# A decode block of attention and gated layer on one core: short on-chip loops on every engine, and the model dimension in four chunks of 112

## The chip, the cores and the metric

One core of a Trainium2 chip runs the whole program. The metric is the device time of one execution in microseconds, the median over several runs; a profiled execution gives the trace. Engines are named as the profile names them: PE (matmuls), DVE (vector), ACT (activations), POOL, and SP, which here only issues loads.

## What is computed

A pre-norm decode step for B = 2 rows with one new token each: attention over a cache of 8192 keys and values for 16 heads of 256, then a gated layer without a nonlinearity. Model dimension D = 448, inner dimension F = 1792, everything in float32.

```python
def _A_ref(x, k_cache, v_cache, wq, wo):
    q = (x @ wq).reshape(B, Sq, H, Dh).transpose(0, 2, 1, 3)
    scores = jnp.einsum("bhqd,bhkd->bhqk", q, k_cache) * (Dh ** -0.5)
    p = _softmax(scores, axis=-1)
    o = jnp.einsum("bhqk,bhkd->bhqd", p, v_cache)
    return o.transpose(0, 2, 1, 3).reshape(B, Sq, H * Dh) @ wo

def _B_ref(x, w_gate, w_up, w_down):
    h = jnp.einsum("bsd,df->bsf", x, w_gate) * jnp.einsum("bsd,df->bsf", x, w_up)
    return jnp.einsum("bsf,fd->bsd", h, w_down)

h = x + _A_ref(_layernorm(x), A_k_cache, A_v_cache, A_wq, A_wo)
h2 = h + _B_ref(_layernorm(h), B_w_gate, B_w_up, B_w_down)
```

Keys and values are 2 x 16 x 8192 x 256 numbers each, 537 MB of 4-byte numbers in sum; all weights together are much less. Every one of them is read once.

## The kernel before, in words

**A turn.** There are NQ = 32 pairs of head and row, called i in the code. For each, 8192 keys lie on 128 partitions, 64 a partition. DVE multiplies the keys with the query, which is spread to all partitions, in place (L334) and adds up along the 256 (L337), both in two pieces of HC = 16 and 48 keys a partition; then it takes the maximum per partition (L381). PE turns that column (L422), DVE takes the maximum of it (L343), PE spreads it (L426), ACT makes the exponentials p and their sums (L355), PE adds those up (L431), DVE takes the reciprocal (L348). The mix (L413) is 32 matmuls of two columns of p with 512 numbers of v, into four column groups of PE; ACT copies the result (L363), PE folds it (L438), and ACT scales it into oT (L365).

**Buffers and order.** Keys have two buffers, values have one (`v_sb`). SP issues all large loads in the order of the program (L383 to L393): keys i+1 once DVE has the maxima of i-1, then values i once PE has ended the mix of i-1. They are carried out one after the other. wq lies in the buffer of the values at first, so the first values wait for the last matmul of the query projection (L282).

**Programs.** `Line` gives an engine its instructions one by one, so DVE, ACT and SP have the 32 turns written out. `Tensor` records PE's instructions and emits 31 turns as one loop on the chip (L446 to L453), with waits on `turn * by + n`. Turn 31 stands behind the loop.

**The last turn and the rest.** wo is loaded into the buffer of the keys once the maxima of turn 30 are there, and PE adds heads 0 to 14 times wo onto x in a bank of PSUM (`acc_ps`, L493). DVE copies the sums (L513), and PE puts them into two other banks (L523): `h_ps`, from which the second norm is made, and `y_ps`, the output. The last values come in two loads of LASTV = 48 and 16 keys a partition. The last head's product with wo is then added to `h_ps` (L589) and, later, to `y_ps` (L697). The norm's mean and its subtraction go through DVE, ACT and PE (L597 to L620), and DVE spreads the result to `xr` (L630). Gate (L668) and up (L668, in two halves) follow, their product (L717), its turn (L720, L727), and the product with wd into `y_ps` (L738), which DVE copies (L747) and SP stores. The loads of gate, up and wd stand last on SP's queue: gate and up wait for the maxima of turn 31 (L469), wd for the first 48 of the last mix (L547).

**Chunks.** D = 448 is three chunks of 128 and one of 64. So that loads have 128 partitions, the host puts the 64-row chunk of one half of the columns on partitions 0 to 63 and that of the other half on 64 to 127; `LAYOUT` and a fifth column of `xr` and `xz` with zeros serve this.

Of the kernel before, what the change touches and what calls it, by code (L numbers as in the profile page):

```python
# [9 lines left out]
EPS = 1e-5  # L10
P = 128
HALF = 64
DC = 4
YN, YW = 4, D // 4
# [7 lines left out]
LASTV = 48  # L22

FG = (512, 512, 384, 384)
FO = (0, 512, 1024, 1408)
NF = F // P
FH = FG[0] // 2
WIDE = [[min(n, (k + 1) * FH) - k * FH for n in FG] for k in range(2)]
PACKED = [3 * sum(n) + n[0] + n[2] for n in WIDE]
# [3 lines left out]
LAYOUT = (  # L33
    (slice(0, P), slice(0, DC - 1), slice(0, DC - 1)),
    (slice(0, HALF), slice(DC - 1, DC), slice(DC - 1, DC)),
    (slice(HALF, P), slice(DC - 1, DC), slice(DC, DC + 1)),
)


class Line:  # L40


    def __init__(self, nc, engine, name):
        self.e = engine
        self.sem = nc.alloc_semaphore(name=name)
        self.n = 0
        self.seen = {}

    def wait(self, *tokens):
        for sem, n in tokens:  # L50
            if self.seen.get(sem.num, 0) < n:
                self.e.wait_ge(sem, n)
                self.seen[sem.num] = n

    def did(self, ins):
        ins.then_inc(self.sem, 1)
        self.n += 1
        return self.sem, self.n


class Tensor:


    def __init__(self, nc):
        self.e = nc.tensor
        self.sem = nc.alloc_semaphore(name="pe")
        self.n = 0
        self.parts = [(None, [])]

    def loop(self, *turns):  # L70

        self.parts.append((turns or None, []))

    def do(self, make, *waits, inc=False):
        self.parts[-1][1].append((make, waits, inc))
        if inc:
            self.n += 1
            return self.sem, self.n

    def emit(self):  # L80
        for turns, ops in self.parts:
            if turns:
                with self.e.Fori(*turns) as turn:
                    self.emit_part(ops, turn)
            else:
                self.emit_part(ops, None)

    def emit_part(self, ops, turn):
        seen = {}
        for make, waits, inc in ops:  # L90
            for w in waits:
                sem, n = w[:2]
                if len(w) == 3:
                    self.e.wait_ge(sem, turn * w[2] + n)
                elif seen.get(sem.num, 0) < n:
                    self.e.wait_ge(sem, n)
                    seen[sem.num] = n
            ins = make() if turn is None else make(turn)
            if inc:
                ins.then_inc(self.sem, 1)  # L100


def decode_block(nc, x, k_cache, v_cache, wq, wo, wg, wu, wd, out):
# [6 lines left out]
    bank = [nc.alloc_psum_tensor(f"bank{i}", [P, 512], F32)[:] for i in range(8)]  # L110
    first_sem = nc.alloc_semaphore(name="dve_first")
    V = Line(nc, nc.vector, "dve")
    A = Line(nc, nc.scalar, "act")
    A_q = Line(nc, nc.scalar, "act_q")
    G = Line(nc, nc.gpsimd, "pool")
    S = Line(nc, nc.sync, "sp")
    T = Tensor(nc)

# [3 lines left out]
    def load(line, dst, src, sem, n=16):  # L122
        line.e.dma_start(dst, src).then_inc(sem, 16)  # L123
        return sem, n
# [5 lines left out]

    room = {"at": 2 * NF * D}

    def late(*shape):

        n = 1
        for k in shape[1:]:
            n *= k
        at = room["at"]
        room["at"] += -(-n // 8) * 8
        assert room["at"] <= NJ * DH  # L140
        got = k_flat[1][: shape[0], at : at + n]
# [15 lines left out]
    xr = sb("xr", P, DC + 1, B, 16)  # L157
    xz = sb("xz", P, DC + 1, B)
    sel = sb("sel", P, 2)
    rep = sb("rep", P, 2, B, REP)  # L160
    q_sb = sb("q_all", B, H * DH)

    s_x, s_wq, s_k0 = landing("x"), landing("wq"), landing("k0")
    s_k = [landing("k_even"), landing("k_odd")]
    s_v, s_v2 = landing("v"), landing("v_last")
    s_wo = [landing("wo_a"), landing("wo_b")]
    s_wg, s_wu = landing("wg"), [landing("wu_a"), landing("wu_b")]
    s_wd = [landing(f"wd{i}") for i in range(len(DOWN))]
    s_out = landing("out")
# [7 lines left out]
    x_in = load(A, x_sb, x.rearrange("b s d -> (b s) d"), s_x)  # L177
    wq_t = v_flat[:, : 3 * H * DH + H * DH // 2]
    wq_in = load(S, wq_t, wq, s_wq)
    k0_in = load(S, k_sb[0][:, :HC], keys_of(k_cache, 0, 0, HC), s_k0)  # L180
    k_in = {0: load(S, k_sb[0][:, HC:], keys_of(k_cache, 0, HC, NJ), s_k[0])}
    k_in[1] = load(S, k_sb[1], keys_of(k_cache, 1, 0, NJ), s_k[1])

    zero = G.did(nc.gpsimd.memset(ident, 0.0))
    G.wait(zero)
    ident_in = G.did(
        nc.gpsimd.affine_select(
            out=ident, in_=ident, compare_op=ALU.not_equal, fill=1.0, base=0,
            pattern=[[-1, P]], channel_multiplier=1,
        )  # L190
    )
    G.did(nc.gpsimd.memset(xz, 0.0))
    zeros_in = G.did(nc.gpsimd.memset(xr[:, DC - 1 :], 0.0))

    V.did(nc.vector.memset(eps_t, EPS))
    V.did(nc.vector.memset(ones, 1.0))
    V.did(nc.vector.memset(avg, 1.0 / D))
    V.did(nc.vector.memset(row, DH**-0.5))
    o_ps, h_ps, y_ps = bank[0], bank[5][:, :P], bank[6][:, :YW]
    V.wait(x_in)  # L200
    xsum = sb("xsum", B, 1)
    t = V.did(nc.vector.tensor_reduce(xsum, x_sb, axis=AX.X, op=ALU.add))
    V.wait(t)
    xmean = sb("xmean", B, 1)
    t = V.did(nc.vector.tensor_scalar(xmean, xsum, -1.0 / D, None, op0=ALU.mult))
    V.wait(t)
    xc_sb = sb("xc", B, DC * P)
    t = V.did(nc.vector.tensor_scalar(xc_sb[:, :D], x_sb, xmean, None, op0=ALU.add))
    V.wait(t)
    xc_in = V.did(nc.vector.tensor_copy(xc_sb[:, D:], xc_sb[:, D - HALF : D]))  # L210
    xq = o_sb[:B, :D]
    t = V.did(nc.vector.tensor_mul(xq, xc_sb[:, :D], xc_sb[:, :D]))
    V.wait(t)
    xvar = sb("xvar", B, 1)
    var_in = V.did(nc.vector.tensor_reduce(xvar, xq, axis=AX.X, op=ALU.add))

    std = sb("std", B, 1)
    A.wait(var_in)
    std_in = A.did(nc.scalar.activation(std, xvar, AF.Sqrt, bias=eps_t, scale=1.0 / D))
    rstd = sb("rstd", B, 1)  # L220
    V.wait(std_in)
    rstd_in = V.did(nc.vector.reciprocal(rstd, std))
    A.wait(rstd_in)
    A.did(nc.scalar.activation(std, std, AF.Exp, scale=0.0))

    xT_ps = bank[3][:, : DC * B].rearrange("p (c b) -> p c b", b=B)
    for c in range(DC):
        xT_in = T.do(
            lambda c=c: nc.tensor.transpose(
                xT_ps[:, c, :], xc_sb[:, c * P : (c + 1) * P], ident[:B, :B]  # L230
            ),
            ident_in, xc_in, inc=c == DC - 1,
        )
    V.wait(xT_in, zeros_in)
    for rows, c, to in LAYOUT:
        xz_in = V.did(nc.vector.tensor_copy(xz[rows, to], xT_ps[rows, c]))

    V.wait(ident_in)
    V.did(
        nc.vector.tensor_reduce(  # L240
            sel, ident.rearrange("p (g r) -> p r g", r=32)[:, :2, :], axis=AX.X, op=ALU.add
        )
    )
    V.did(
        nc.vector.tensor_copy(
# [4 lines left out]
    for ps in (o_ps, h_ps, bank[4][:, :HW]):  # L250
        set_in = V.did(nc.vector.memset(ps, 0.0))

    q_sel = sb("q_sel", B, DH)
    qb = [sb(f"qb{i}", P, DH) for i in range(2)]
    qb_ps = bank[1][:, :DH]
    q_ps = [bank[7][:B, :], bank[4][:B, :]]
    qsel_in, qb_in, Q_in = {}, {}, {}

    def select(i):
        h, b = divmod(i % NQ, B)  # L260
        if i > 0:
            A.wait(Q_in[i - 1])
        qsel_in[i] = A_q.did(
            nc.scalar.activation(  # L264
                q_sel, q_sb[:, h * DH : (h + 1) * DH], AF.Copy, scale=ident[:B, b : b + 1]
            )
        )

    def spread_query(*_):
        return nc.tensor.matmul(qb_ps, ones[:B, :], q_sel, start=True, stop=True)  # L270

    def take_query(i):
        A.wait(Q_in[i])
        qb_in[i] = A_q.did(nc.scalar.activation(qb[i % 2], qb_ps, AF.Copy))  # L274

    q_in = {}
    for g in range(NG):
        for c in range(DC):
            xs = c if c < DC - 1 else c + g // (NG // 2)
            at = c * H * DH + (g * QG if c < DC - 1 else g % (NG // 2) * QG)  # L280
            done = T.do(
# [536 lines left out]
```

## Time and profile before

| what | value |
|---|---|
| runs, median of 3 | 1302.09 us (1301.49 to 1303.19) |
| profiled execution, its own time | 1301.42 us |
| its span, first to last instruction | 1300.1 us |
| busy: DVE, PE, ACT | 1131.2 us (87%), 470.6 us (36%), 81.5 us (6%) |
| HBM read | 561.19 MB |

In a row of groups stand: line, engine, operation, output and inputs by tile, shapes, how many; behind the first bar the busy time in us and the mean of one in ns; behind the second the idle time of the engine just before them in us and what ended most of it. PEld is PE's loading of weights, SPq the issuing of a load. One float32 matmul of the program shows as two MATMULs and two weight loads. In the timeline the idle time ahead stands in brackets.

### The profile page before, as it was taken

Reading aid. Unit: us, or ns where it says so; the run is one execution under the profiler, and the core shown is the slowest. Engines: PE = TensorE matmul, PEld = TensorE weight load, DVE = VectorE, ACT = ScalarE, POOL = GpSimd, SP = SyncE. Lnnn points to the kernel's source line nnn. Section 1 sums busy time; section 2 is a strip of 40 time slices with the busy share of each in tenths; the row PEclk is TensorE's granted clock in tenths of the full one; section 3 lists DMA queues with packets and bytes.
Section 4 is the critical chain, followed back from the end, with each engine's and each line's share of the span. In section 5 each row is a group of like instructions: output and inputs, shape, how many; then the busy total and the mean of one; then the engine's idle time right before and its main releaser. Section 6 shows DMA issues by size and latency. Waiting matters only on the chain.

```text
span 1300.1 us, 6914 instructions
## 1 busy us (share of the span) xinstructions
PE 470.6 (36%) x2992; PEld 155.1 (12%) x2992; DVE 1131.2 (87%) x266; ACT 81.5 (6%) x239; POOL 0.8 (0%) x8
## 2 busy tenths in 40 slices
PE   3643224333323433322333322333321333432387
PEld 0111011101001101101101101101100110110123
DVE  1999998889888889888889988888988888988861
ACT  1100000000000000000000000000000000000000
POOL 0000000000000000000000000000000000000000
PEclk9866566666556666556666656666656666655689
DMA  9999999999999999999999999999999999999998
GB/s 411 427 450 421 450 421 444 426 436 436 421 450 421 448 423 448 423 446 425 442 427 427 444 421 450 422 446 425 446 423 446 425 440 429 427 444 423 446 421 367
DMA packets 10973, 561.31 MB, mean 432 GB/s; under 512 B 1234, under 2 KB 1364, under 8 KB 1492
## 3 DMA queue, kind: packets, MB, share of 16 engines
q1 hardware_dynamic: 10960, 561.19, 99.7%
q8 instruction: 5, 0.08, 0.0%
q14 instruction: 4, 0.03, 0.0%
q10 hardware_dynamic: 4, 0.00, 0.0%
HBM read 561.19 MB, written 0.00 MB: 432 GB/s over the span
## 4 chain that ended last, share of the span: by engine, by line
DMA 74%; PE 25%; issue 0%; ACT 0%; SPq 0%; DVE 0%
DMA v<-in_A_v_cache_dram 71%; PE bank L413 22%; PE bank L282 2%; DMA v<-in_wd_dram 2%; DMA v<-in_wq_dram 1%; PE bank L270 0%; SPq L123 0%; PE bank L738 0%; ACT q_all L290 0%; ACT q_sel L264 0%; DVE k L747 0%; ACT qb L274 0%
## 5 line engine op out<-in xcount | busy, mean ns | idle before, releaser
L334 DVE TENSOR_TENSOR k<-k,qb 128x4096 f32<-128x4096 f32 x64 | 555.3, 8676 | 124.2 <-DMA k<-in_A_k_cache_dram 95.9
L337 DVE TENSOR_REDUCE s<-k 128x16 f32<-128x4096 f32 x64 | 555.2, 8675 | 1.1
L413 PE MATMUL bank<-v,p 128*2 128x512 f32 x2048 | 291.4, 733 | 342.9 <-DMA v<-in_A_v_cache_dram 342.9
L413 PEld LDWEIGHTS bank<-v,p 128*2 128x2 f32 x2048 | 53.6, 96 | 573.4 <-DMA v<-in_A_v_cache_dram 365.9
L426 PE MATMUL bank<-nm,row 1*128 1x1 f32 x64 | 18.4, 354 | 227.6 <-DVE nm L343 227.6
L422 PE MATMUL bank<-ident,m 128*1 128x128 f32 x32 | 11.8, 368 | 184.4 <-DVE m L381 184.4
L363 ACT ACTIVATE o_sb<-bank 128x512 f32<-128x512 f32 x31 | 18.5, 597 | 604.0 <-PE bank L413 604.0
L426 PEld LDWEIGHTS bank<-nm,row 1*128 1x128 f32 x64 | 15.6, 302 | 236.9 <-DVE nm L343 236.9
L438 PE MATMUL bank<-sel,o_sb 128*128 128x1 f32 x256 | 33.7, 253 | 23.3 <-ACT o_sb L363 22.5
L270 PE MATMUL bank<-q_sel,ones 2*128 2x256 f32 x66 | 39.0, 691 | 1.4 <-ACT q_sel L264 1.4
L438 PEld LDWEIGHTS bank<-sel,o_sb 128*128 128x128 f32 x256 | 31.0, 191 | 53.1 <-ACT o_sb L363 51.5
L282 PE MATMUL bank<-v,xz 128*2 128x512 f32 x64 | 30.7, 639 | 16.0 <-DMA v<-in_wq_dram 16.0
L352 ACT ACTIVATE nb<-bank 128x1 f32<-128x1 f32 x32 | 5.5, 171 | 441.5 <-PE bank L426 441.5
L431 PE MATMUL bank<-lsum,ones 128*128 128x1 f32 x64 | 18.5, 359 | 23.5 <-ACT p L355 23.5
L422 PEld LDWEIGHTS bank<-ident,m 128*1 128x1 f32 x32 | 2.5, 79 | 188.2 <-DVE m L381 187.8
L431 PEld LDWEIGHTS bank<-lsum,ones 128*128 128x128 f32 x64 | 15.8, 306 | 26.2 <-ACT p L355 26.2
L270 PEld LDWEIGHTS bank<-q_sel,ones 2*128 2x128 f32 x66 | 15.9, 297 | 3.7 <-ACT q_sel L264 2.4
L264 ACT ACTIVATE q_sel<-q_all,ident 2x256 f32<-2x256 f32 x33 | 16.2, 492 | 0.0
L274 ACT ACTIVATE qb<-bank 128x256 f32<-128x256 f32 x32 | 12.2, 382 | 54.5 <-PE bank L270 54.5
L493 PE MATMUL bank<-k,oT 128*2 128x224 f32 x120 | 13.4, 387 | 0.0
L343 DVE TENSOR_REDUCE nm<-bank 1x1 f32<-1x128 f32 x32 | 8.7, 272 | 4.4 <-PE bank L422 4.4
L597 DVE TENSOR_REDUCE k<-bank 128x1 f32<-128x128 f32 x1 | 0.3, 292 | 13.1 <-PE bank L589 13.1
(81 smaller groups left out, 97.3 us busy)
## 6 DMA issues: line engine op xcount, KB each, us to landing
v<-in_wq_dram SPq DMA_DIRECT2D x1, 7168.0 KB, 19.5
k<-in_wo_dram SPq DMA_DIRECT2D x2, 3584.0 KB, 35.3
k<-in_A_k_cache_dram SPq DMA_DIRECT2D x1, 6144.0 KB, 38.0
v<-in_A_v_cache_dram SPq DMA_DIRECT2D x1, 6144.0 KB, 21.6
k<-in_wg_dram SPq DMA_DIRECT2D x1, 3136.0 KB, 28.0
v<-in_wd_dram SPq DMA_DIRECT2D x2, 1120.0 KB, 18.0
k<-in_A_k_cache_dram SPq DMA_DIRECT2D x1, 2048.0 KB, 23.9
v<-in_A_v_cache_dram SPq DMA_DIRECT2D x1, 2048.0 KB, 26.1
```

What stands on the lines that cost most here:

```text
L264: nc.scalar.activation(q_sel, q_sb[:, h * DH : (h + 1) * DH], AF.Copy, scale=ident[:B, b : b + 1])
L270: return nc.tensor.matmul(qb_ps, ones[:B, :], q_sel, start=True, stop=True)
L282: lambda g=g, c=c, xs=xs, at=at: nc.tensor.matmul(q_ps[g % 2], xz[:, xs, :], wq_t[:, at : at + QG], start=(c == 0), stop=(c == DC - 1),),
L334: t = V.did(nc.vector.tensor_mul(kt, kt, q[:, None, :].to_broadcast([P, hi - lo, DH])))
L337: V.did(nc.vector.tensor_reduce(s_t[i % 2][:, lo:hi], kt, axis=AX.X, op=ALU.add)),
L363: osb_in[i] = A.did(nc.scalar.activation(o_sb, o_ps, AF.Copy))
L413: lambda *_, t=t, g=g: nc.tensor.matmul(o_ps[g : g + 2, :], p_t[:, 2 * t : 2 * t + 2], v_sb[:, 2 * t : 2 * t + 2, :], start=(t < 4), stop= ...
L422: return T.do(lambda *_: nc.tensor.transpose(mT_ps, m_t, ident), m, inc=True)
L426: lambda *_: nc.tensor.matmul(nb_ps, row, nm, start=True, stop=True), nm_done, inc=True
L431: lambda *_: nc.tensor.matmul(l_ps, ones, lsum, start=True, stop=True), p_done, inc=True
L438: lambda *_, c=c, k=k: nc.tensor.matmul(oT_ps[:, c : c + 1], o_sb[:, (2 * k + c) * P : (2 * k + c + 1) * P], sel[:, k : k + 1], start=(k = ...
L493: lambda h=h, c=c, k=k: nc.tensor.matmul(acc_ps[HALF * k : HALF * k + B, :], oT[:, h, c, :], wo_c[:, h, c, k * HW : (k + 1) * HW], start=F ...
```

## The change

**Loops.** One class `Engine` records the instructions of every engine; each waits for, and signals, names, and counts are worked out afterwards. `roll` emits a stretch as a loop on that engine alone, waiting on `turn * a + b`; `only` puts part of a turn under a test on the turn's number. DVE's turns 1 to 30 become a loop of two turns each, ACT's 32 turns a loop of 16 with two each (the spread of queries 32 to 34 is made, too, and not used), PE's query projection a loop of four, and PE's 32 turns a loop that now holds the last turn, whose extra work stands under tests. SP's loads stay written out.

**Chunks.** D is four chunks of W = 112, so wq, gate and up lie on 112 partitions with rows longer by 128/112; `LAYOUT` and the zeros go. Gate is loaded in two halves, and the groups of F are 512, 512, 512, 256.

**The last head.** It joins the other heads in `acc_ps`; ACT copies the sums once and adds them up on the way; both `xc_ps` and `y_ps` are made from that copy. The last values come in loads of 40, 16 and 8, and wd waits for the end of the mix.

```diff
-LASTV = 48
+LAST = (40, 16, 8)
-FG = (512, 512, 384, 384)
+FG = (512, 512, 512, 256)
-DC = 4
-YN, YW = 4, D // 4
+DC, W = 4, D // 4
...
+    def roll(self, lo, hi, step, body):
+        steps = range(lo, hi, step)
+        self.items.append(["roll", steps, [self.inner(body, i) for i in steps]])
+    def only(self, here, body, *args):
+        self.items.append(["only", self.inner(body, *args) if here else []])
...
+                with self.nc.Fori(
+                    steps.start, steps.stop, steps.step, engines=[self.e.engine]
+                ) as turn:
+                    self.emit_turn(turns, steps, turn, known, {})
...
+                here = turn < steps[1] if at == [0] else turn > steps[-2]
+                with self.e.If(here):
+                    self.emit_ops(turns[at[0]][k][1], known, {})
...
+                self.e.wait_ge(sem, turn * a + b if a else b)
...
+    wq_t = v_flat[:W, : DC * H * DH]
+    wg_t = k_flat[1][:W, : DC * F]
+    wu_t = k_flat[1][:W, DC * F : 2 * DC * F]
...
-    v_in = load(S, v_sb[:, :LASTV], keys_of(v_cache, n, 0, LASTV), s_v, 16 * NQ)
-    v2_in = load(S, v_sb[:, LASTV:], keys_of(v_cache, n, LASTV, NJ), s_v2)
+    for k, n in enumerate(LAST):
+        load(
+            S, v_sb[:, at : at + n], keys_of(v_cache, NQ - 1, at, at + n),
+            s_v if k == 0 else landing(f"v_last{k}"),
+            ("v", NQ - 1) if k == 0 else ("v_last", k), ("M", NQ - 2), n=16 * NQ if k == 0 else 16,
+        )
+    for k, part in enumerate((slice(0, GC), slice(GC, DC * F))):
+        load(S, wg_t[:, part], wg[:, part], landing(f"wg{k}"), ("wg", k), ("m", NQ - 1))
...
-    S.wait(mixed_a)
+            landing(f"wd{k}"), ("wd", k), ("M", NQ - 1),
...
+    T.roll(0, NG // 2, 1, project_groups)
+    spread_query(1)
...
+    V.roll(1, NQ - 1, 2, lambda i: (scores(i), scores(i + 1)))
+    scores(NQ - 1)
...
+    A.roll(0, H, 1, act_turn)
...
+    def tensor_turn(i):
+        last = i == NQ - 1
+        T.only(last, heads_out, 0)
...
+        T.only(last, heads_out, 1)
+        at = 0
+        for k, n in enumerate(LAST):
+            if k > 0:
+                T.only(last, hold, ("v_last", k))
+            mix(
+                i, at, at + n, *([("v", i)] if k == 0 else []),
+                done=("M", i) if k == len(LAST) - 1 else None,
+            )
...
+    T.roll(0, NQ, 1, tensor_turn)
+    project_out(H - 1, H, ("oT", NQ - 1), done="acc")
+    A.do(
+        lambda: nc.scalar.activation(sums, acc_ps, AF.Copy, accum_out=total), "acc", done="sums"
+    )
...
+    V.do(
+        lambda: nc.vector.tensor_copy(xr, xc_ps[:, :, :, None].to_broadcast([W, DC, B, REP])),
+        "xc_h", done="xr",
+    )
```

On PE, in the loop over turns, before: from the spread of the query to the back edge (L413 is the mix, L438 the fold).

```order
L270 MATMUL bank<-q_sel,ones 128x256
L94 ISA
L413 MATMUL bank<-v,p 2x512 x32
L94 REGISTER_ALU
L438 MATMUL bank<-sel,o_sb 128x1 x4
L83 REGISTER_ALU
L83 COMPARE_AND_BRANCH
```

The same place in the changed program, from behind the spread of the query to the end of the mix (L511 is the product with wo of the last turn, L498 the mix).

```order
L110 COMPARE_AND_BRANCH
L511 MATMUL bank<-k,oT 2x224 x28
L110 UNCONDITIONAL_BRANCH
L129 ISA
L498 MATMUL bank<-v,p 2x512 x20
L110 COMPARE_AND_BRANCH
L110 UNCONDITIONAL_BRANCH
L498 MATMUL bank<-v,p 2x512 x8
L110 COMPARE_AND_BRANCH
L110 UNCONDITIONAL_BRANCH
L498 MATMUL bank<-v,p 2x512 x4
L129 REGISTER_ALU
```

The mix is cut in three, with tests between, and 60 matmuls with wo and two with x now stand in the loop's body, jumped over in all turns but the last.

On DVE, one head of the turns written out, before (the names in brackets are the counters waited for: pe is PE's, dve its own, k_odd the landing of keys).

```order
L334 TENSOR_TENSOR k<-k,qb 128x4096 [waits act_q,k_odd]
L343 TENSOR_REDUCE nm<-bank 1x1 [waits pe]
L337 TENSOR_REDUCE s<-k 128x16 [waits dve]
L348 RECIPROCAL rl<-bank 128x1 [waits pe]
L334 TENSOR_TENSOR k<-k,qb 128x12288
L337 TENSOR_REDUCE s<-k 128x48 [waits dve]
L381 TENSOR_REDUCE m<-s 128x1 [waits dve]
```

The same for the first of the two heads in DVE's loop of the changed program.

```order
L129 ISA [waits k_odd]
L409 TENSOR_TENSOR k<-k,qb 128x4096 [waits act1]
L129 ISA
L437 TENSOR_REDUCE nm<-bank 1x1 [waits pe0]
L129 ISA
L418 TENSOR_REDUCE s<-k 128x16 [waits dve0]
L129 REGISTER_ALU
L442 RECIPROCAL rl<-bank 128x1 [waits pe0]
L409 TENSOR_TENSOR k<-k,qb 128x12288
L129 REGISTER_ALU
L418 TENSOR_REDUCE s<-k 128x48 [waits dve0]
L129 REGISTER_ALU
```

The operations and their order are the same (the maximum per partition, L431, follows); register instructions that work out the counts to wait for stand between them, 14 in a turn of two heads with the loop's own.

On PE behind the last mix, before (L438 folds, L589 is the last head times wo, L613 and L620 take off the mean, L668 is gate).

```order
L413 MATMUL bank<-v,p 2x512 x32
L438 MATMUL bank<-sel,o_sb 128x1 x4
L589 MATMUL bank<-k,oT 2x128 x8
L613 MATMUL bank<-k,ones 128x8
L620 MATMUL bank<-ident,k 128x8
L668 MATMUL bank<-k,xr 32x512 x2
```

And in the changed program (L511 is the last head times wo, L583 and L594 take off the mean, L600 opens `y_ps`, L637 is gate).

```order
L498 MATMUL bank<-v,p 2x512 x4
L129 REGISTER_ALU
L564 MATMUL bank<-sel,o_sb 128x1 x4
L95 REGISTER_ALU
L95 COMPARE_AND_BRANCH
L511 MATMUL bank<-k,oT 2x224 x4
L583 MATMUL bank<-ident,k 112x4 x2
L594 MATMUL bank<-k,ones 112x8
L600 MATMUL bank<-k,rep 32x112 x4
L637 MATMUL bank<-k,xr 32x512 x3
```

Four matmuls of the last head stand where eight stood, and what L523 and L697 did for `y_ps` is now L600, behind the mean.

More of the change, by code (lines that the diff above doesn't have):

```diff
@@ L40 @@
[L40 to L84, printed above, removed]
-            else:
[L86 to L100, printed above, removed]
@@ new lines, in decode_block @@
+    load_k(0, lo=HC)
+    load_k(1)
+    for i in range(NQ):
+        if 2 <= i + 1 < NQ:
+            load_k(i + 1, ("m", i - 1))
+        if i < NQ - 1:
+            load(
+                S, v_sb, keys_of(v_cache, i, 0, NJ), s_v, ("v", i),
+                "all_q" if i == 0 else ("M", i - 1), n=16 * (i + 1),
+            )
+    cut = H * D
+    for k in range(2):
+        part = slice(k * cut, (k + 1) * cut)
+        load(S, wo_t[:, part], wo[:, part], landing(f"wo{k}"), ("wo", k), ("m", NQ - 2))
@@ L193, in decode_block @@
[L193 to L205, printed above, removed]
@@ L220, in decode_block @@
[L220 to L233, printed above, removed]
@@ L234, in decode_block @@
[L234 to L245, printed above, removed]
+        ),
+        "zero", done="ident",
+    )
+    for t, value in ((eps_t, EPS), (ones, 1.0), (avg, 1.0 / D), (row, DH**-0.5)):
+        V.do(lambda t=t, value=value: nc.vector.memset(t, value))
@@ new lines, in spread_query, with project_groups @@
+    def spread_query(i, name="Q"):
+        T.do(
+            lambda *_: nc.tensor.matmul(qb_ps, ones[:B, :], q_sel, start=True, stop=True),
+            ("qsel", i), done=(name, i),
+        )
+    def project_groups(t):
+        for k in range(2):
+            for c in range(DC):
+                T.do(
+                    lambda turn, k=k, c=c: nc.tensor.matmul(
+                        q_ps[k], xz[:, c, :],
+                        wq_t[:, bass.ds(turn * (2 * QG) + (c * H * DH + k * QG), QG)],
+                        start=(c == 0), stop=(c == DC - 1),
+                    ),
+                    *([("q", 2 * (t - 1) + k)] if c == 0 else []),
+                    done=("qp", 2 * t + k) if c == DC - 1 else None,
+                )
+        T.only(t == 0, spread_query, 0, "Q0")
@@ L402, in every, with collect @@
-    def every(tokens):
-        sem, n = tokens[0]
-        by = tokens[1][1] - n
-        assert all(tokens[i] == (sem, n + by * i) for i in range(TURNS)), tokens
-        return sem, n, by
-    def mix(lo, hi, landed):
+            ),
+            ("nb", i), done=("p", i),
+        )
+    def collect(i, turn_of):
+        b = i % B
+        A.do(lambda *_: nc.scalar.activation(o_sb, o_ps, AF.Copy), ("M", i), done=("osb", i))
+        A.do(
+            lambda turn: nc.scalar.activation(
+                oT[:, bass.ds(turn_of(turn), 1), :, b], oT_ps[:, None, :], AF.Copy, scale=rl
+            ),
+            ("O", i), ("rl", i), done=("oT", i),
+        )
@@ L410, in mix, with act_turn @@
+    def act_turn(h):
+        for b in range(B):
+            i = h * B + b
+            exponentials(i)
+            take_query(i + 2)
+            select(i + 3, lambda turn, b=b: (turn + (b + 3) // B) & (H - 1))
+            collect(i, lambda turn: turn)
+    A.roll(0, H, 1, act_turn)
+    def mix(i, lo, hi, *waits, done=None):
         for t in range(lo // 2, hi // 2):
             g = 32 * (t % 4)
-            done = T.do(
+            T.do(
                 lambda *_, t=t, g=g: nc.tensor.matmul(
@@ L434, in turn_up, with project_out @@
-    def turn_up(o_done):
+    def project_out(lo, hi, *waits, done=None):
+        for h in range(lo, hi):
+            for c in range(2):
+                for k in range(2):
+                    last = h == hi - 1 and c == k == 1
+                    T.do(
+                        lambda h=h, c=c, k=k: nc.tensor.matmul(
+                            acc_ps[HALF * k : HALF * k + B, :], oT[:, h, c, :],
+                            wo_c[:, h, c, k * HW : (k + 1) * HW],
+                            start=False, stop=(h == H - 1 and c == 1),
+                        ),
+                        *(waits if h == lo and c == k == 0 else []), done=done if last else None,
+                    )
@@ new lines, in heads_out, with hold @@
+    def heads_out(k):
+        if k == 0:
+            for j in range(2):
+                T.do(
+                    lambda j=j: nc.tensor.matmul(
+                        acc_ps[HALF * j : HALF * j + B, :], ident[:B, :B],
+                        x_sb[:, j * HW : (j + 1) * HW], start=True, stop=False,
+                    )
+                )
+            project_out(0, H // 2, ("wo", 0), ("oT", H - 1))
+        else:
+            project_out(H // 2, H - 1, ("wo", 1), ("oT", NQ - 3))
+    def hold(*waits):
+        T.do(None, *waits)
@@ L441, in turn_up @@
                     ),
-                    o_done, inc=c == k == 1,
-                )
-        return done
-    T.loop(0, TURNS)
-    find_top(every(m_in))
-    spread_top(every(nm_in))
-    add_up(every(p_in))
-    T.do(spread_query, every({i: qsel_in[i + 2] for i in range(TURNS)}), inc=True)
-    mix(0, NJ, (s_v, 16, 16))
-    turn_up(every(osb_in))
-    T.loop()
-    T.n = first + PER * TURNS
-    n = NQ - 1
-    wo_t = k_flat[0][:, : 2 * H * D]
-    cut = H * D
-    S.wait(m_in[n - 1])
-    wo_in = [
-        load(S, wo_t[:, k * cut : (k + 1) * cut], wo[:, k * cut : (k + 1) * cut], s_wo[k])
-        for k in range(2)
-    ]
@@ L545, in decode_block @@
-    last["M"] = mix(LASTV, NJ, v2_in)
-    S.wait(mixed_a)
-    wd_t = v_flat[:, : NF * D].rearrange("p (n d) -> p n d", d=D)
-    wd_in, at = {}, 0
-    for k, cnt in enumerate(DOWN):
-        got = load(
-            S, wd_t[:, at : at + cnt, :].rearrange("p n d -> p (n d)"),
-            wd[:, at * D : (at + cnt) * D], s_wd[k],
-        )
-        for j in range(at, at + cnt):
-            wd_in[j] = got
-        at += cnt
-    A.wait(last["M"])
-    osb_in[n] = A.did(nc.scalar.activation(o_sb, o_ps, AF.Copy))
@@ L647, in decode_block @@
[L647 to L674 removed]
+                    *([("osb", i)] if c == k == 0 else []),
@@ new lines, in tensor_turn @@
+                    done=("O", i) if c == k == 1 else None,
+                )
+    T.roll(0, NQ, 1, tensor_turn)
+    project_out(H - 1, H, ("oT", NQ - 1), done="acc")
+    sums, total, mean = late(P, HW), late(P, 1), late(P, DC, B)
+    A.do(
+        lambda: nc.scalar.activation(sums, acc_ps, AF.Copy, accum_out=total), "acc", done="sums"
+    )
+    for j in range(2):
+        T.do(
+            lambda j=j: nc.tensor.matmul(
+                xc_ps[:, 2 * j : 2 * j + 2, :], sums[:, j * W : (j + 1) * W],
+                ident.rearrange("p (k r) -> p k r", k=2)[:, :, :B], start=(j == 0), stop=False,
+            ),
+            "sums",
+        )
@@ new lines, in decode_block @@
+    V.do(
+        lambda: nc.vector.tensor_mul(mean, share, total[:, None, :].to_broadcast([P, DC, B])),
+        "sums", "share", done="mean",
+    )
+    T.do(
+        lambda: nc.tensor.matmul(xc_ps, ones[:, :W], mean, start=False, stop=True),
+        "mean", done="xc_h",
+    )
+    for q in range(DC):
+        T.do(
+            lambda q=q: nc.tensor.matmul(
+                y_ps[32 * q : 32 * q + 32, :], rep[:, q // 2].rearrange("p b r -> p (b r)"),
+                sums[:, q % 2 * W : (q % 2 + 1) * W], start=True, stop=False,
+            )
+        )
```

787 lines of the change are left out of this document (350 added, 437 removed).

## The prediction

> **What bounds the kernel now.** I read the page first, then the chain of waits in order of time, then the DMA issues, then the timeline of the last 50 us.
>
> The page: the DMA row of the 40 slices, the queues (packets, MB, share of the 16 DMA engines' span), the chain by engine, and the three costliest groups.
>
> ```profile
> span 1300.1 us, 6914 instructions
> ...
> DMA  9999999999999999999999999999999999999998
> ...
> q1 hardware_dynamic: 10960, 561.19, 99.7%
> q8 instruction: 5, 0.08, 0.0%
> q14 instruction: 4, 0.03, 0.0%
> ...
> HBM read 561.19 MB, written 0.00 MB: 432 GB/s over the span
> ...
> L334 DVE TENSOR_TENSOR k<-k,qb 128x4096 f32<-128x4096 f32 x64 | 555.3, 8676 | 124.2 <-DMA k<-in_A_k_cache_dram 95.9
> L337 DVE TENSOR_REDUCE s<-k 128x16 f32<-128x4096 f32 x64 | 555.2, 8675 | 1.1
> L413 PE MATMUL bank<-v,p 128*2 128x512 f32 x2048 | 291.4, 733 | 342.9 <-DMA v<-in_A_v_cache_dram 342.9
> ```
>
> The data queue is busy for 99.7% of the sixteen engines' span. What it is not is 0.3% of 1300.1, or 3.9 us. DVE, the next busiest, still idles 95.9 us on keys that have not landed, about 3.0 us for each of 32 heads (a "head" here is one of the 32 pairs of head and batch row); PE idles 342.9 us on values.
>
> The chain (start, us, what) tells where those 3.9 us lie, and the rate:
>
> ```profile
> 0.73 19.49 DMA v<-in_wq_dram
> ...
> 35.68 0.69 PE bank L270 x2
> 36.37 17.27 PE bank L282 x40
> 53.64 0.02 issue
> 53.66 24.57 DMA v<-in_A_v_cache_dram
> ...
> 1200.06 0.04 issue
> 1200.10 8.76 PE bank L413 x64
> 1208.86 0.02 issue
> 1208.88 29.81 DMA v<-in_A_v_cache_dram
> 1238.69 0.04 issue
> ...
> 1277.04 19.87 DMA v<-in_wd_dram
> 1296.91 0.04 issue
> 1296.95 1.02 PE bank L738 x32
> ```
>
> The last weights land at 1296.91, so 3.2 us of the span lie behind them (matmuls, a copy, the store), and the first 0.73 us lie ahead of the first issue. That is all the queue is not busy: nothing between is lost. Values land at 1200.06 and at 1238.69, 38.63 us apart. The sizes:
>
> ```profile
> v<-in_wq_dram SPq DMA_DIRECT2D x1, 7168.0 KB, 19.5
> ...
> v<-in_A_v_cache_dram SPq DMA_DIRECT2D x1, 6144.0 KB, 21.6
> k<-in_wg_dram SPq DMA_DIRECT2D x1, 3136.0 KB, 28.0
> ...
> v<-in_A_v_cache_dram SPq DMA_DIRECT2D x1, 2048.0 KB, 26.1
> k<-in_wu_dram SPq DMA_DIRECT2D x1, 1792.0 KB, 31.9
> k<-in_wu_dram SPq DMA_DIRECT2D x1, 1344.0 KB, 34.6
> ```
>
> One head's values are 6144 + 2048 = 8192 KB and its keys as much, so a head is 16384 KB in 38.63 us: 424.1 KB a us, 19.3 us for keys or values. The change moves the same bytes. So only three things can move the time: the rate of the queue, a hole in it, or the 3.2 us behind it.
>
> **The change part by part.** The sum is made on the profiled execution (span 1300.1, time 1301.42); the median of the runs is 1302.09, 0.67 above it, so I add the change to the median.
>
> *The tail.* Its rows (the timeline before; in brackets the idle time ahead and what ended it):
>
> ```profile
> 1270.35 7.05 PE L413 MATMUL bank<-v,p 128*2 128x512 f32 x64 [3.11 <-DMA v<-in_A_v_cache_dram]
> ...
> 1275.18 0.10 PEld L413 LDWEIGHTS bank<-v,p 128*2 128x2 f32 x4 [0.44 <-DMA v<-in_A_v_cache_dram]
> ...
> 1278.11 1.05 PE L438 MATMUL bank<-sel,o_sb 128*128 128x1 f32 x8 [0.72 <-ACT o_sb L560]
> ...
> 1279.52 0.62 PE L589 MATMUL bank<-k,oT 128*2 128x128 f32 x16 [0.35 <-ACT oT L563]
> ...
> 1281.40 0.57 DVE L630 COPY xr<-bank 128x96 f32<-128x96 f32 x3 [0.60 <-PE bank L620]
> ...
> 1282.58 0.20 PEld L668 LDWEIGHTS bank<-k,xr 128*32 128x32 f32 x8 [1.31 <-DMA k<-in_wg_dram]
> ...
> 1290.01 0.57 PEld L668 LDWEIGHTS bank<-k,xr 128*32 128x32 f32 x16 [0.36 <-DMA k<-in_wu_dram]
> ...
> 1293.46 0.42 DVE L727 COPY k<-bank 128x256 f32<-128x256 f32 x1 [0.53 <-PE bank L720]
> ```
>
> The mix took 7.05 us for 64 matmuls, 0.11 each. With parts of 40, 16 and 8 the last data still land at 1275.2, and only 8 matmuls (0.9 us) follow: the mix ends at 1276.1, not 1277.4. The joint sum then needs 8 matmuls in place of 16 (0.3 us for 0.62), one evacuation with a sum on ACT in place of a reduce and a copy, and one copy to xr in place of three (about 0.25 us for 0.57). So xr is ready near 1280.3, not 1282.0. But the second gate matrix half lands at 1282.58 whatever xr does, and the second half of up at 1290.01; behind that stands the same short run of matmuls, product, flip and copy, which ended at 1293.46 + 0.42 = 1293.9. The last of wd lands at 1296.91. So the gain of 1.7 us widens a cover of 3.0 us and the end doesn't see it: 0. If xr were instead up to 3 us late, still 0.
>
> *Loops on DVE and ACT.* A DVE turn of two heads gains 14 register instructions and a back edge. DVE before has no such row. The nearest is PE, whose loop already waits on a register for its values: the 0.04 us of issue at 1200.06 and 1238.69, between landing and first matmul. 15 x 0.04 = 0.6 us for two heads, against 2 x 3.0 us that DVE spends waiting for keys. Bounds: 0 (hidden behind the long instructions ahead of them) to 15 x 0.19 = 2.9 us, if each cost a whole small copy (L630, 0.57 us for three); both are under 6.0. Cost on the path: 0. If the cover were gone, every microsecond past it would come back 16 times.
>
> *PE's turn.* It gains four tests that jump over work of the last head, two of them between pieces of the mix. What is queued behind them is the rest of the mix, then SP's load of the next values, which waits for the whole mix into the single buffer v. That load is issued at 1208.88 and lands 29.81 us later, of which 19.3 us are its transfer: for 10.5 us it stands behind the keys. Four tests are 0.2 us at 0.04 us each, and 2.9 us if each cost a whole matmul (L413's mean, 733 ns). Hidden either way: 0.
>
> *Projection of the queries.* wq has the same 7168 KB, the matmuls are as many. The second spread (0.69 us at 35.68) goes behind the loop, four turns' edges come in. What this gates is the first load of values, issued at 53.66. Ahead of it the queue holds wq, landed at 0.73 + 19.49 = 20.22, and two heads' keys, 16384 KB or 38.6 us: until 58.8. Cover 5.2 us, against at most 4 x 0.73 - 0.69 = 2.2 us. 0 again.
>
> *The wait of wd.* Its loads now wait for the whole last mix (1276.1) rather than for its first 48 chunks. Only the output queues behind them on SP. They can't start before gate and up are through, 3136 + 1792 + 1344 = 6272 KB or 14.8 us after 1275.2: 1290.0. Cover 13.9 us: 0.
>
> *Code from HBM.* The two instruction queues brought 0.11 MB in nine packets. With loops on DVE and ACT most of the four on q14 should go and q8 lose one or two. Spread over 16 engines the 0.11 MB are 0.11 / 432 = 0.26 us; if all sat on one of them (27 GB/s) and that one ended last, 4.1 us. Not all go; I take -0.5 us, near the spread end. From below, nothing or a little: a gain can't be excluded, a loss is a rival below.
>
> *112 rows in place of 128* for wq, wg and wu: 7168 + 6272 = 13440 KB, 31.7 us at 424.1. Rows are longer by 128/112, and 112 is 16 x 7, so sixteen engines can take seven rows each: then 0. No row of before has such a load. The other end: if a row's share of the rate is what is fixed, the three take 8/7 of 31.7 us, +4.5 us.
>
> [...]
>
> I take 0: in the rows above equal bytes take equal time (keys, values, weights with long or short rows: 6272 KB from 1275.2 to 1290.0 are 424 KB a us as well), which looks like a limit of each engine that seven equal rows would not change.
>
> Sum: -0.5 us on 1302.1: **1301.6**.
>
> **The rivals.**
>
> *The 112 rows cost (slower).* Place: wq's landing, and the gate and up loads; price +4.5 - 0.5 = +4.0: 1306.1. It decides as soon as the engines' writes into SBUF, not the engines, are the limit. For it: all loads run at the same 424 KB a us, a hard limit, and the trace doesn't say whether it sits ahead of SBUF or at it. Against: the even sharing above. 0.19.
>
> [...]
>
> *PE's loop no longer fits where its code is kept (slower).* PE's body grows from 40 matmuls to 102. Each is two MATMULs and two weight loads (L413: 2048 for 1024 in the program), so 160 instructions become 408; the 316 matmuls of PE's whole program, 1264 instructions, came in q8's five packets if those are PE's, 253 to a packet. If each turn fetched them again, 32 turns at 1.6 packets of 16 KB are 0.84 MB, 2 us over sixteen engines, 31 us if one carries them: up to 1333. Against: 31 turns of before needed five packets in all. [...] 0.03.
>
> *DVE or PE outgrow their cover (slower).* DVE from 3.0 us a head on, PE from 10.5 us: one more microsecond a head is 32 us: 1334. Bounds above speak against. 0.03.
>
> *The code packets were worth their 4.1 us (faster):* 1298.0. It needs all nine on one engine and all gone. 0.05.
>
> *The change doesn't do what it says:* packets on q14 stay four; then it is 1302.1, inside the forecast's own case.
>
> **How the numbers follow.** About 0.2% (2.6 us) is what a measurement of this kernel can tell from no change. The forecast's case has 0.61 and lies in 1300 to 1303, all within 0.2%. Slower: 0.19 + 0.09 + 0.03 + 0.03 = 0.34. Faster: 0.05. The range reaches from 1300.0 over the 112-row case at 1306.1, and the 0.7 us between profiled run and median, to 1306.8; what is left out is 0.09 + 0.03 + 0.03 + 0.05 = 0.20.
>
> **What would show it.** Right: the data queue again at 99.6% or more, wq landing within 0.5 us of 20.2, gate and up taking 14.8 us between the last values and the last up half, xr ready ahead of the second gate half, the last weights landing some 3.2 us before the end, fewer packets on q14. Wrong in size: wq landing 2.4 us late and gate and up 2.1 us longer (the 112 rows), or far more (collisions). Wrong in kind: instruction packets in the hundreds, DVE no longer waiting for keys, or PE's mix no longer waiting for values.

## The result, and the profile after

The changed kernel took 1332.84 us (median of 6, 1329.41 to 1338.52) against 1302.05 us before: a ratio of 1.0239, with an interval of 1.0216 to 1.0263. Run again beside other kernels it took 1332.21 us. The forecast of 1301.6 us, no change, was wrong: the time lies 26 us above the top of its range, 1306.8. Of the kernel with wq alone on 112 rows, below, one of four runs took 1342.88 us and the others 1315.36 to 1316.20; its time and ratio are those of the three.

The profiled execution took 1334.07 us, its span 1332.7. Of its page, the rows that answer to those of before: rate by slice, queues, bytes, chain, DVE's and PE's groups (L409, L418 and L498 are the old L334, L337 and L413).

```profile
span 1332.7 us, 7584 instructions
...
DMA  9999999999999999999999999999999999999997
GB/s 232 439 431 439 435 435 429 435 439 431 439 429 435 439 431 439 425 439 439 431 437 427 439 439 431 437 425 441 439 431 437 425 441 437 433 435 427 432 350 201
...
q1 hardware_dynamic: 11168, 561.19, 99.4%
q8 instruction: 3, 0.05, 0.0%
q14 instruction: 3, 0.02, 0.0%
...
HBM read 561.19 MB, written 0.00 MB: 421 GB/s over the span
...
L409 DVE TENSOR_TENSOR k<-k,qb 128x4096 f32<-128x4096 f32 x64 | 555.3, 8676 | 137.7 <-DMA k<-in_A_k_cache_dram 98.3
L418 DVE TENSOR_REDUCE s<-k 128x16 f32<-128x4096 f32 x64 | 555.2, 8675 | 1.1
L498 PE MATMUL bank<-v,p 128*2 128x512 f32 x2048 | 291.7, 733 | 350.7 <-DMA v<-in_A_v_cache_dram 350.7
```

The rate by slice before:

```profile
GB/s 411 427 450 421 450 421 444 426 436 436 421 450 421 448 423 448 423 446 425 442 427 427 444 421 450 422 446 425 446 423 446 425 440 429 427 444 423 446 421 367
```

The same bytes, and a queue that is called busy for 99.4% of a span that is 32.6 us longer. No other row has grown by as much: DVE waits 98.3 us for keys (95.9 before), PE 350.7 us for values (342.9). What has changed is the rate, and only at the two ends: 232 GB/s in the first slice (411 before), 350 and 201 in the last two (421 and 367). A busy queue is not a fast one.

The same in stretches, before (us of the stretch, its length, busy time and count of each engine, granted clock, DMA share, GB/s):

```profile
2.00:20.00 18.00, 0.56 (x4) 0.50 (x4) 4.12 (x15) 2.37 (x4) 0.00 (x0) 1.00 0.88 380
...
60.00:1180.00 1120.00, 374.42 (x2292) 122.30 (x2292) 1026.36 (x205) 65.07 (x203) 0.00 (x0) 0.61 1.00 434
```

and after:

```profile
2.00:20.00 18.00, 0.50 (x4) 0.44 (x4) 3.52 (x11) 2.48 (x5) 0.00 (x0) 1.00 1.00 255
20.00:34.00 14.00, 0.00 (x0) 0.00 (x0) 0.00 (x0) 0.00 (x0) 0.00 (x0) 1.00 0.86 200
...
60.00:1180.00 1120.00, 374.62 (x2263) 121.82 (x2264) 1026.31 (x205) 66.27 (x205) 0.00 (x0) 0.61 1.00 434
```

The 1120 us in the middle are the same to the GB/s. In the first 34 us, while wq is landing, the queue moves 200 to 255 GB/s. The chain of waits dates the landing:

```profile
0.74 33.80 DMA v<-in_wq_dram
```

34.54 in place of 20.22: 14.3 us. The tail, from its timeline:

```profile
1290.54 1.04 PE L498 MATMUL bank<-v,p 128*2 128x512 f32 x8 [1.51 <-DMA v<-in_A_v_cache_dram]
...
1298.09 0.29 DVE L606 COPY xr<-bank 112x128 f32<-112x128 f32 x1 [1.18 <-PE bank L594]
...
1305.16 0.20 PEld L637 LDWEIGHTS bank<-k,xr 112*32 112x32 f32 x8 [2.57 <-DMA k<-in_wg_dram]
...
1319.97 0.20 PEld L637 LDWEIGHTS bank<-k,xr 112*32 112x32 f32 x6 [3.77 <-DMA k<-in_wu_dram]
...
1325.53 5.05 PE L690 MATMUL bank<-v,k 128*32 128x112 f32 x112
```

From the last part of the values on, gate and up take 1319.97 - 1290.54 = 29.4 us to land, 1290.01 - 1275.18 = 14.8 before. And the 112 matmuls with wd, which used to wait piece by piece for wd, now stand in one block behind the last flip, because up came so late that wd was there first, all but its last pieces. The 3.2 us behind the last weights no longer set the end.

### The profile page after: what moved, and what is told of

Read it like the earlier page. It is cut to its first block, busy times and chain, and to the rows that moved or that the text cites. A ratio compares the mean times of both kernels' runs of the same rounds, so it can differ in the third digit from the quotient of the medians.

```text
span 1332.7 us, 7584 instructions
## 1 busy us (share of the span) xinstructions
PE 481.4 (36%) x2952; PEld 159.1 (12%) x2952; DVE 1129.6 (85%) x255; ACT 83.4 (6%) x245; POOL 0.7 (0%) x6
## 3 DMA queue, kind: packets, MB, share of 16 engines
q1 hardware_dynamic: 11168, 561.19, 99.4%
## 4 chain that ended last, share of the span: by engine, by line
DMA 50%; DVE 40%; issue 8%; PE 2%; another core or an unknown queue 0%; DVEq 0%; ACT 0%; SPq 0%
DMA k<-in_A_k_cache_dram 44%; DVE s L418 21%; DVE k L409 18%; DMA k<-in_wu_dram 3%; DMA v<-in_wq_dram 3%; PE bank L350 1%; PE bank L637 1%; PE bank L690 0%; DVE m L431 0%; DVE nm L437 0%; DVE rl L442 0%; DVEq L129 0%; PE bank L670 0%; ACT q_all L366 0%
## 5 line engine op out<-in xcount | busy, mean ns | idle before, releaser
L409 DVE TENSOR_TENSOR k<-k,qb 128x4096 f32<-128x4096 f32 x64 | 555.3, 8676 | 137.7 <-DMA k<-in_A_k_cache_dram 98.3
L418 DVE TENSOR_REDUCE s<-k 128x16 f32<-128x4096 f32 x64 | 555.2, 8675 | 1.1
L498 PE MATMUL bank<-v,p 128*2 128x512 f32 x2048 | 291.7, 733 | 350.7 <-DMA v<-in_A_v_cache_dram 350.7
L498 PEld LDWEIGHTS bank<-v,p 128*2 128x2 f32 x2048 | 53.6, 97 | 581.5 <-DMA v<-in_A_v_cache_dram 371.8
L540 PE MATMUL bank<-ident,m 128*1 128x128 f32 x32 | 11.8, 370 | 175.4 <-DVE m L431 175.4
L350 PE MATMUL bank<-v,xz 112*2 x64 | 30.2, 633 | 30.7 <-DMA v<-in_wq_dram 30.7
L564 PEld LDWEIGHTS bank<-sel,o_sb 128*128 128x128 f32 x256 | 31.7, 194 | 53.1 <-ACT o_sb L473 53.1
L637 PE MATMUL bank<-k,xr 112*32 112x256 f32 (+1 forms) x88 | 14.8, 749 | 10.0 <-DMA k<-in_wu_dram 7.5
L377 ACT ACTIVATE q_sel<-q_all,ident 2x256 f32 (+1 forms) x35 | 17.2, 492 | 0.0
L511 PE MATMUL bank<-k,oT 128*2 128x224 f32 x128 | 15.0, 398 | 0.5 <-ACT oT L475 0.5
```

What stands on the lines that cost most here:

```text
L350: lambda turn, k=k, c=c: nc.tensor.matmul(q_ps[k], xz[:, c, :], wq_t[:, bass.ds(turn * (2 * QG) + (c * H * DH + k * QG), QG)], start=(c == ...
L377: return nc.scalar.activation(q_sel, q_sb[:, bass.ds(at, DH)], AF.Copy, scale=ident[:B, b : b + 1])
L409: lambda *_: nc.vector.tensor_mul(kt, kt, q[:, None, :].to_broadcast([P, hi - lo, DH])),
L418: lambda *_: nc.vector.tensor_reduce(s[:, lo:hi], kt, axis=AX.X, op=ALU.add),
L498: lambda *_, t=t, g=g: nc.tensor.matmul(o_ps[g : g + 2, :], p_t[:, 2 * t : 2 * t + 2], v_sb[:, 2 * t : 2 * t + 2, :], start=(t < 4), stop= ...
L511: lambda h=h, c=c, k=k: nc.tensor.matmul(acc_ps[HALF * k : HALF * k + B, :], oT[:, h, c, :], wo_c[:, h, c, k * HW : (k + 1) * HW], start=F ...
```

## The experiments

Three theories were set against each other. Theory A: loads onto 112 partitions run at about half the rate, and the rest of the change costs nothing. Theory B: the loops, the tests or the later wait of wd cost it. Theory C: 112 rows cost 8/7, and the rest lies elsewhere.

**The change with 128-row loads of the same bytes.** In the host's packing, and the tiles, halves and column places to match:

```diff
-        return a.transpose(1, 0, 2).reshape(W, -1)
+        return a.transpose(1, 0, 2).reshape(P, -1)
...
-    wq_t = v_flat[:W, : DC * H * DH]
+    wq_t = v_flat[:, : DC * H * DH * W // P]
```

> The changed kernel, but wq, gate and up are loaded as 128 rows of 7/8 of the length (same bytes, same number of loads); the numbers then lie in other places than the matmuls take them from, so the output is not the reference's, and instructions, waits and bytes are those of the change. Theory A (a load onto 112 partitions runs at about half the rate, and nothing else of the change costs anything): 1301 to 1303 us, wq landing at 20.2 us. Theory B (the loops, the test jumps or the later wait of wd cost it, the slow loads are only filled time): 1320 to 1334 us. Theory C (112 rows cost 8/7 and the rest comes from elsewhere): 1328 us, 4.5 us less than the change.

Measured: 1301.66 us, ratio 0.9998 (0.9989 to 1.0007). From its chain and its timeline:

```profile
0.74 19.54 DMA v<-in_wq_dram
...
50.95 28.29 DMA v<-in_A_v_cache_dram
...
1297.03 0.04 issue
```

```profile
1275.38 1.04 PE L499 MATMUL bank<-v,p 128*2 128x512 f32 x8 [0.55 <-DMA v<-in_A_v_cache_dram]
...
1278.70 0.93 PE L512 MATMUL bank<-k,oT 128*2 128x224 f32 x8 [0.52 <-ACT oT L476]
...
1281.06 0.29 DVE L607 COPY xr<-bank 112x128 f32<-112x128 f32 x1 [0.74 <-PE bank L595]
...
1293.54 0.42 DVE L678 COPY k<-bank 128x256 f32<-128x256 f32 x1 [0.53 <-PE bank L672]
...
1297.08 0.97 PE L692 MATMUL bank<-v,k 128*32 128x112 f32 x32 [0.40 <-DMA v<-in_wd_dram]
```

All 31 us are gone: theories B and C fall. Loops, tests, joint sum, three loads of the last values and the wait of wd together cost nothing that can be measured, and bring nothing. wq lands at 20.28, the first values are issued at 50.95, the last weights land at 1297.03.

**The change with rows of zeros.** 16 rows of zeros are added to wq, gate and up; the matmuls still read 112:

```diff
-        return a.transpose(1, 0, 2).reshape(W, -1)
+        a = a.transpose(1, 0, 2).reshape(W, -1)
+        return np.concatenate([a, np.zeros((P - W, a.shape[1]), a.dtype)], axis=0)
```

> The changed kernel with 16 rows of zeros added to wq, gate and up, so that these loads have 128 rows of the changed length: 1920 KB more bytes, output unchanged. Theory A: 1302 + 4.5 = 1306 to 1308 us, wq landing at 22.6 us. Theory B: 1333 + 4.5 = 1337 us. Theory C (each row has a fixed share): no difference from the change, 1333 us.

Measured: 1306.25 us, ratio 1.0031 (1.0019 to 1.0043). 1920 KB more make the kernel 26.6 us faster than the change is. Theory A had forecast that; wq landed at 0.74 + 21.95 = 22.69.

**The kernel before with wq alone on 112 rows.**

```diff
-    wq_t = v_flat[:, : 3 * H * DH + H * DH // 2]
+    wq_t = v_flat[:YW, : DC * H * DH]
...
-            xs = c if c < DC - 1 else c + g // (NG // 2)
-            at = c * H * DH + (g * QG if c < DC - 1 else g % (NG // 2) * QG)
+            xs = c
+            at = c * H * DH + g * QG
```

> The kernel before, with wq alone in four chunks of 112 rows (its load, the query projection and the first norm's chunks); no loops added, gate and up as before. Theory A: the 14.3 us by which wq landed later with the change come back whole, 1316 us, wq landing at 34.5 us. Theory B: 1302 us. Theory C: 1304.5 us.

Measured: 1315.52 us, ratio 1.0105 (1.0086 to 1.0123): 13.6 us, without a single new loop. (The 13.9 in the expectations further down goes by the median of all four runs, 1315.86.) The chain has the landing of its wq at 34.23:

```profile
0.73 33.50 DMA v<-in_wq_dram
```

**Only loads, by the number of partitions.**

```python
ROWS = (128, 112, 96, 80, 64, 48, 32, 16)
for i, rows in enumerate(ROWS):
    s.dma_start(big[i % 2][:rows, :], flat[i, :rows, :]).then_inc(done, 16)
    n += 16
    s.wait_ge(done, n)
```

> Only loads of keys, nothing computed: 64 KB a partition onto 128, 112, 96, 80, 64, 48, 32 and 16 partitions from partition 0 on, each waiting for the one ahead. If the number of partitions sets the rate (a fixed share for each): all eight take the same 19.3 us or so. If sixteen engines share any number of rows evenly: times in proportion to rows, 19.3, 16.9, 14.5, 12.1, 9.7, 7.2, 4.8, 2.4 us plus a constant. If engines writing to the same group of partitions halve each other: 128 rows 19.3 us; 112 rows 33 us (as in the change); 64 rows or fewer at half the rate or less, 64 rows 19.3 us, 32 rows 9.7 us, 16 rows 9.7 us if four engines meet at a place. If anything but 128 rows falls to half the rate: 33.8, 29, 24, 19.3, 14.5, 9.7, 4.8 us from 112 down.

Each load ran once. The stretches run from each load's first packet to the end of its last, in that order; the last columns are the DMA share and GB/s.

```profile
1.76:22.20 20.44, 0.00 (x0) 1.00 0.97 407
23.52:54.82 31.30, 0.00 (x0) 1.00 0.96 232
56.30:86.90 30.60, 0.00 (x0) 1.00 0.97 206
88.39:114.07 25.68, 0.00 (x0) 1.00 0.96 204
116.36:137.23 20.87, 0.00 (x0) 1.00 0.97 201
138.98:164.02 25.04, 0.00 (x0) 1.00 0.95 126
165.59:176.44 10.85, 0.00 (x0) 1.00 0.92 193
178.23:187.85 9.62, 0.00 (x0) 1.00 0.83 102
```

128 rows take 20.4 us; 112 rows, fewer bytes, 31.3 us. At 96, 80, 64 and 32 rows the rate is about 200 GB/s, but 126 at 48 and 102 at 16. No rule by number alone fits, neither a fixed share a row nor a flat half: 48 rows take longer than 64. The share of busy time is 0.92 to 0.97, and 0.83 at 16 rows: the engines are occupied, not idle.

**Only loads, by place.** The same loop with other partitions. Each load reads neighbouring rows from the first on, but of another pair of head and row (`flat[i]`), so the source is alike and not the same.

```python
PLACES = (
    (112, 0, 1), (112, 16, 1), (16, 0, 1), (16, 0, 4), (16, 0, 8),
    (8, 0, 1), (8, 0, 4), (8, 0, 16), (128, 0, 1),
)
...
to = big[i % 2][first : first + (rows - 1) * step + 1 : step, :]
```

> Only loads of keys, nothing computed, each waiting for the one ahead, 64 KB a partition; the source rows are the same contiguous ones, only the partitions differ. Order: 112 partitions from 0 on; 112 from 16 on; 16 partitions 0 to 15; 16 partitions 0, 4, 8 to 60; 16 partitions 0, 8, 16 to 120; 8 partitions 0 to 7; 8 partitions 0, 4 to 28; 8 partitions 0, 16 to 112; 128 partitions. [...] Theory N (the number of rows in the load sets the rate, not their place): the three loads of 16 take the same 9.6 us, and the three of 8 the same time as each other. Theory S (the source rows sit in the memory so that engines meet there): the same as N, since the source does not change with the place.

```profile
1.75:33.23 31.48, 0.00 (x0) 1.00 0.96 231
34.68:67.68 33.00, 0.00 (x0) 1.00 0.92 220
69.20:78.44 9.24, 0.00 (x0) 1.00 0.94 113
81.21:86.77 5.56, 0.00 (x0) 1.00 0.85 189
88.64:94.29 5.65, 0.00 (x0) 1.00 0.81 174
95.90:104.86 8.96, 0.00 (x0) 1.00 0.46 59
107.58:110.81 3.23, 0.00 (x0) 1.00 0.44 162
112.52:117.82 5.30, 0.00 (x0) 1.00 0.44 99
119.58:140.33 20.75, 0.00 (x0) 1.00 0.97 404
```

Sixteen rows take 9.2 us on partitions 0 to 15 and 5.6 us when spread by four; eight rows take 9.0, 3.2 and 5.3 us on three places. Bytes and number of rows are the same, and the place decides, by a factor of 2.8. That each load reads another pair of head and row makes little of it: with place and rows alike, the two kernels of loads give 31.3 and 31.5 us for 112 rows, 9.6 and 9.2 for 16, 20.4 and 20.8 for 128. So N and S fall. That engines hold each other up where they write is the author's idea of the cause; no run shows it.

What a row costs an engine can be estimated from the lines: length times busy share times 16, by the number of rows. That is 2.5 us at 128 rows and 2.8 for eight rows spread by four; 4.3 at 112 rows and 4.6 to 4.7 for sixteen rows spread by four or eight and for eight spread by 16; 8.2 to 8.7 for eight or sixteen neighbours. In the loads by number it is 4.9 to 5.1 us at 96, 80, 64 and 32 rows, 7.9 at 48 and 8.0 at 16. The 31.3 us of 112 rows compare with 17.9, seven eighths of the 20.4 us of 128 rows.

Why is not shown. Eight or sixteen neighbours by themselves cost 8.2 to 8.7 us a row, and 128 rows, neighbours as well, 2.5. Which rows an engine takes no run shows, so why a row costs 4.3 us at 112 rows and 2.5 at 128 stays open.

**The change with the tail alone on 112 rows.** Zeros for wq only.

```diff
-    got["wq"] = rows(wq)
+    zeros = np.zeros((P - W, DC * H * DH), wq.dtype)
+    got["wq"] = np.concatenate([rows(wq), zeros], axis=0)
```

> The changed kernel with 16 rows of zeros added to wq alone, output unchanged: the projection's load has 128 rows, gate and up keep 112. If head and tail add up: 1301.7 + 2.3 (zeros) + 17.3 (31.2 by which the change is slower than the same with 128-row loads, less 13.9 that wq alone cost) = 1321 us. If only the doubled transfer of gate and up counts, without the matmuls at the end that then come late: 1301.7 + 2.3 + 14.8 = 1319 us. If the late wq also delays the tail of the changed kernel, so that the tail is less without it: below 1317 us.

Measured: 1316.94 us, ratio 1.0124 (1.0107 to 1.0141). The median is just inside the third case, but the four runs reach from 1316.45 to 1320.40 and don't part it from the second. The zeros, 1024 KB, are 2.4 us at 424.1 KB a us; above 1301.66 + 2.4 the tail alone costs 12.9 us.

```profile
1279.06 1.04 PE L498 MATMUL bank<-v,p 128*2 128x512 f32 x8 [1.67 <-DMA v<-in_A_v_cache_dram]
...
1305.34 1.06 PE L637 MATMUL bank<-k,xr 112*32 112x256 f32 x12 [1.85 <-DMA k<-in_wu_dram]
...
1312.01 0.97 PE L690 MATMUL bank<-v,k 128*32 128x112 f32 x32 [0.43 <-DMA v<-in_wd_dram]
```

Gate and up land in 1305.34 - 1279.06 = 26.3 us here, not 29.4, and the end again waits for wd, 3.1 us ahead of the span's end at 1315.1.

**The change with the head alone on 112 rows, and the change again.** The counterpart, with zeros for gate and up:

```diff
-    got["wg"] = rows(gate, TURNED)
+    got["wg"] = np.concatenate([rows(gate, TURNED), zeros], axis=0)
...
-    got["wu"] = np.concatenate(parts, axis=1)
+    got["wu"] = np.concatenate([np.concatenate(parts, axis=1), zeros], axis=0)
```

> The counterpart of the run with the tail alone: 16 rows of zeros added to gate and up, wq on 112 rows, output unchanged. If head and tail add up apart from a remainder that needs both slow loads: 1301.7 + 2.1 (zeros) + 13.9 (wq alone in the kernel before) = 1317.7 us. If the changed kernel's loops make a late wq dearer than it is in the kernel before: the 4 us that head and tail leave unexplained lie here, 1322 us.

Measured: 1316.73 us, ratio 1.0110 (1.0093 to 1.0127). So the head costs 1316.73 - 1301.66 - 2.1 = 13.0 us in the changed kernel, no more than the 13.6 in the kernel before: the loops don't make it dearer.

> The changed kernel once more, beside the run with the head alone on one chip. 1329 to 1338 us as in its first six runs, if its spread is its own; a narrower spread around one value if the spread was that of the chips.

Measured: 1332.21 us (1331.14 to 1334.36), ratio 1.0227 (1.0210 to 1.0244). Beside it the head alone spread from 1316.57 to 1317.37, by 0.8 us; the change spreads by 3.2 here, and the tail alone spread by 4.0. So the spread goes with slow loads of gate and up, as far as four runs each can tell, and not with a slow wq.

Head 13.0 and tail 12.9 leave some 5 us of the 31.2 that need both. The profiles show where they are: gate and up 29.4 us against 26.3, and 12.7 us from the last up half to the end (1319.97 to 1332.7) against 9.8 (1305.34 to 1315.1), together 6.0 us. The second profile of the change has both again: 1321.20 - 1290.62 = 30.6 us, and 11.8 us from there to its end at 1333.0.

```profile
1290.62 1.04 PE L498 MATMUL bank<-v,p 128*2 128x512 f32 x8 [2.63 <-DMA v<-in_A_v_cache_dram]
...
1321.20 0.20 PEld L637 LDWEIGHTS bank<-k,xr 112*32 112x32 f32 x6 [4.46 <-DMA k<-in_wu_dram]
```

In that last stretch PE was granted 0.54 of its clock in the change and 1.00 with the tail alone (the clock is the column ahead of the DMA share):

```profile
1320.00:1331.00 11.00, 10.04 (x140) 6.50 (x140) 1.55 (x4) 0.00 (x0) 0.00 (x0) 0.54 0.35 144
```

```profile
1305.30:1312.00 6.70, 5.13 (x108) 3.04 (x108) 1.27 (x3) 0.00 (x0) 0.00 (x0) 1.00 0.78 319
```

In the kernel before, the 112 matmuls with wd took 1.17 + 1.17 + 0.97 = 3.3 us at a clock of 1.00. Their 5.05 us in the change go with a clock of 0.54 in that stretch; what lowered it no run shows. Why gate and up are slower behind a slow wq was not tried.

## Why the prediction was wrong, point by point

The step that failed is "*112 rows in place of 128* ... I take 0". It reasoned that equal bytes take equal time "which looks like a limit of each engine that seven equal rows would not change". All rows it rested on had 128 partitions, and so could not tell a limit of the engines from one of the places that they write to; the prediction said so itself ("No row of before has such a load", and, of the limit, "the trace doesn't say whether it sits ahead of SBUF or at it") and still chose the kind end. In its place: wq took 33.8 us for 19.5, gate and up 29.4 us for 14.8, and the same bytes on 128 rows gave the whole 31 us back.

The upper bound of that step, +4.5 us, failed too. It let each row's share set the time. By that 112 or 96 rows of 64 KB would take no longer than 128; they took 31.3 and 30.6 us for 20.4. A count of rows is not enough: eight rows took 3.2, 5.3 or 9.0 us by their place. What makes the place count no run shows.

The 0.09 among the slower chances, "collisions" in the prediction's last paragraph, is for engines that meet where they write. No run shows such a meeting; what the runs showed in its place is that the loads take 1.7 times as long (wq, 33.8 us for 19.5) to twice as long (gate and up, 29.4 for 14.8). Doubling 31.7 us would have given 1301.6 + 31.7 = 1333.3, close to the 1332.84 measured, but partly by luck: each end by itself costs 13 us, 26 together, and the rest came with slower loads of gate and up behind a late wq (29.4 us for 26.3) and with PE's clock (0.54 for 1.00).

Two other rivals named the right time for a wrong reason: 1333 for PE's code and 1334 for DVE or PE past their cover. The profile refutes both. The instruction queues brought three packets each, fewer than before, and DVE waited 98.3 us for keys. A time that fits is not yet a cause.

What held, by the run with 128-row loads: the loops (the middle runs at 434 GB/s as before); the first load of values, issued at 50.95 where 53.66 was early enough; wd, whose wait never showed; the cover at the end. The copy behind its last flip ended at 1293.54 + 0.42 = 1293.96, forecast 1293.9, and the last weights came at 1297.03. xr was ready at 1281.35, not 1280.3: the joint product took 0.93 us (from 1278.70) where 0.3 was reckoned, and nothing came of it, since the cover was there. The 0.3 took the halved number of matmuls and overlooked that each is longer, 224 numbers for 128; those of heads 0 to 14 in the kernel before (L493), with 224, took 13.4 us for 120, 0.11 each. The code packets fell from nine to six, and the 0.5 us that they were to bring lie within what can be told (1301.66 beside 1301.97).

## What to carry to other kernels

Take a row of a profile as a bound for a new load only if the load has the same shape on the chip: the 407 GB/s measured here on 128 partitions were 232 on 112. When a change keeps bytes and alters the number of partitions, time the load by itself first; here one kernel of eight loads would have shown the price. And a queue's share of busy time can't be read as its speed (0.97 and 0.96 in those two loads): look at GB/s by slice or stretch beside it. Where a load has 112 rows, filling it up to 128 with zeros can pay: here 1920 KB of them saved 26.6 us.

## What the runs showed of the hardware

A load's place can count as much as its size: eight rows of 64 KB land in 3.2 us on one set of partitions and in 9.0 on another, and moving 112 rows up by 16 partitions changes little (31.5 and 33.0 us). A load of fewer rows can take longer: 48 rows 25.0 us, 64 rows 20.9, and 112 rows 31.3 for the 20.4 of 128.
